# The first two units of a fused attention, mix and expert kernel, written as one fixed list of steps

## The chip, the core and the metric

The kernel runs on one core of a Trainium2 chip. The metric is the time of one execution on the device, in microseconds (us). The engines of the core are named as in the profile: PE (TensorE, matrix products), DVE (VectorE), ACT (ScalarE), POOL (GpSimd) and SP (SyncE, which here only issues transfers). Each engine works through its own list of instructions in order; semaphores hold an instruction back until what it reads is there, or until the buffer that it writes is free.

## What is computed

Three blocks follow each other; everything is float32, but for the three weights `w_k`, `w_v` and `w_r` of the second block, which come as float64.

```python
# 1: attention inside chunks of 64 tokens; q, k, v are 8 x 8 heads x 576 tokens x 64
scores = scale * np.matmul(q_c, k_c.transpose(0, 1, 2, 4, 3))
attn = np.exp(scores - scores.max(-1)); attn /= attn.sum(-1) + 1e-09
x = np.matmul(attn, v_c)                       # -> 8 x 576 x 512
# 2: each token mixed with the one before it, then a gated two-layer net
xk = mu_k * x + (1.0 - mu_k) * x_prev
xr = mu_r * x + (1.0 - mu_r) * x_prev
k = np.maximum(xk @ w_k, 0.0)                  # w_k 512 x 1024
v = k * k @ w_v                                # w_v 1024 x 512
x = v / (1.0 + np.exp(-(xr @ w_r)))            # w_r 512 x 512
# 3: four experts, causal attention each, the two best per token (not touched by the change)
```

## The kernel before

The 4608 tokens are cut into 36 tiles of 128 (two of them are a pair) and into 12 units of 384 tokens (three tiles). Block 1 is done pair by pair: `s_T` transposes a q and a k tile on PE (L148), `s_S` makes the scores of a pair (L185) and its softmax on DVE and ACT (row maximum L190, subtraction L191, exponential L194, sum L196 to L198, multiplication L199), `s_PT` transposes the result and `s_PV` multiplies it with v (L219) and copies it into `XT`, the attention's result of a unit.

Block 2 is done unit by unit. `s_shift` makes the two mixed inputs in four parts of 128 channels: ACT scales the token before (L268), DVE adds the token itself (L269), ACT rounds the sum to the high half (L270), DVE subtracts to get the low half (L271). Every product of this block is taken as three matmuls of 384 columns (high by high, high by low, low by high; L57 to L59 in `mm3`), so a unit takes 48 matmuls for r (4 output blocks), 96 for k (8 blocks) and 96 for v (4 blocks in two halves). The result of k is squared and split by ACT (L294 to L296) and, in the first two units, by DVE (L297).

The float64 weights are turned into pairs of float32 halves while the first units run: 20 chunks of 128 x 512 numbers (4 of `w_r`, 8 of `w_k`, 8 of `w_v`), each loaded as 512 KB of raw words (L328) into the tile `st`. A chunk goes through a chain over three engines: absolute value on ACT (L334), maximum with a small constant on POOL (L335), a shift and two bit operations on DVE (L336 to L338), rounding to the high half on POOL (L46), and the subtraction for the low half on DVE (L348).

What is issued when is set in two steps. The code's order comes from the string `pro` (a chunk `c`, an attention step `a`, loads `q` and `v`) and then from the loop over units, which puts conversions (`early`), attention steps (`rate0`, `rate`) and shifts (`sh`, `sh2`) between the blocks of r, k and v. Then the scheduler of the language reorders instructions inside each engine's list by priority and by its own timing. From unit 2 on there are no conversions any more, only r, k, v, attention and shifts; after unit 11 the experts follow.

Of the kernel before, what the change touches and what calls it, by code (L numbers as in the profile page):

```python
# [61 lines left out]
def attn_mix(tc, at, x2T, q, k, v, mu_k, mu_r, w_k, w_v, w_r, ident, attended_all, mixed_k):  # L62
# [14 lines left out]
    with ExitStack() as ctx:  # L77
# [24 lines left out]
        def load_qk(t):  # L102
            for src, nm in ((q, "q"), (k, "k")):
                if by_dve(t):
# [39 lines left out]
        def to_sbuf(src, nm):  # L144

            p = bank("Tps")
            for g in range(HP):
                nc.tensor.transpose(p[:, g], src[:, g * 128:(g + 1) * 128], ident)  # L148
            o = at.tile([128, HP, 128], F32, tag=nm, bufs=CFG["tb"], name=nm)
            nc.scalar.activation(out=o, in_=p, func=ACTF.Copy)  # L150
            return o

# [15 lines left out]

        def s_S(j):
# [15 lines left out]
            m = at.tile([128, 2, 2, HP], F32, tag="m", name="m")  # L187
            e = at.tile([128, 2, HP, 2, CH], F32, tag="P", name="P")
            for o, p in enumerate(banks):
                nc.vector.tensor_reduce(m[:, o], p, axis=AXX, op=ALU.max)  # L190
                nc.vector.tensor_tensor(e[:, :, :, o], p, m[:, o].unsqueeze(3).to_broadcast([128, 2, HP, CH]),  # L191
                                        op=ALU.subtract)
            ef = e.rearrange("p i g o k -> p (i g o) k")
            nc.scalar.activation(out=ef, in_=ef, func=ACTF.Exp, scale=scale)  # L194
            z = m.rearrange("p o i g -> p (o i g)")
            nc.vector.tensor_reduce(z, ef, axis=AXX, op=ALU.add)  # L196
            nc.vector.tensor_scalar(z, z, 1e-9, None, op0=ALU.add)
            nc.vector.reciprocal(z, z)  # L198
            eng(nc, CFG["amul"][j >= CFG["first_j"]]).tensor_tensor(  # L199
                ef, ef, z.unsqueeze(2).to_broadcast([128, 2 * H, CH]), op=ALU.mult)  # L200
            for i in range(2):
                PP[2 * j + i] = e[:, i]

        def s_PV(j):
            banks = [bank("PVps").rearrange("p g (i k) -> p i g k", i=2) for _ in range(2)]
# [15 lines left out]
            for c, p in enumerate(banks):  # L221

                done = 0
                while done < 2:
# [32 lines left out]
        def s_shift(u, ws, g):  # L257
            x = XT[u]
            now, prev = x[:, g, :, 1:], x[:, g, :, :SEG]
            for w in ws:  # L260
                nm = "kr"[w]
                if g == 0:
                    XS[u, w] = Split(wkr.tile([128, KD, UNIT], F32R, tag="xh" + nm, name="xh" + nm),
                                     wkr.tile([128, KD, UNIT], F32R, tag="xl" + nm, name="xl" + nm))
                o = XS[u, w]
                a = wkr.tile([128, NSEG, SEG], F32, tag="xa", bufs=2, name="xa")
                af = a.rearrange("p s t -> p (s t)")
                nc.scalar.activation(out=a, in_=prev, func=ACTF.Copy, scale=mu1[:, w, g:g + 1])  # L268
                nc.vector.scalar_tensor_tensor(a, now, mu[:, w, g:g + 1], a, op0=ALU.mult, op1=ALU.add)  # L269
                nc.scalar.activation(out=o.hi[:, g], in_=af, func=ACTF.Copy)  # L270
                nc.vector.tensor_tensor(o.lo[:, g], af, f32(o.hi[:, g]), op=ALU.subtract)  # L271
# [6 lines left out]
        def mix_r(u, m):  # L278
            if m == 0:
                sig[u] = mx.tile([128, KD, UNIT], F32, tag="sig", name="sig")  # L280
            p = ps.tile([128, UNIT], F32, tag="mix", bufs=3, name="mps")
            cc = slice(m * 128, (m + 1) * 128)
            mm3(nc, p, [((wr.hi[:, g, cc], wr.lo[:, g, cc]), rhs(XS[u, 1], g)) for g in range(KD)])
            nc.scalar.activation(out=sig[u][:, m], in_=p, func=ACTF.Sigmoid)  # L284

        def mix_k(u, m):
            p = ps.tile([128, UNIT], F32, tag="mix", bufs=3, name="mps")
            cc = slice(m * 128, (m + 1) * 128)
            mm3(nc, p, [((wk.hi[:, g, cc], wk.lo[:, g, cc]), rhs(XS[u, 0], g)) for g in range(KD)])
            o = Split(mx.tile([128, UNIT], F32R, tag="kh", bufs=KF, name="kh"),  # L290
                      mx.tile([128, UNIT], F32R, tag="kl", bufs=KF, name="kl"))
            r2 = wkr.tile([128, UNIT], F32, tag="r2", bufs=2, name="r2")
# [9 lines left out]
        def mix_v(u, m, half):
            if half == 0:
                vps[0] = ps.tile([128, UNIT], F32, tag="mix", bufs=3, name="mps")
            p = vps[0]
            cc = slice(m * 128, (m + 1) * 128)
            gs = range(half * KF // 2, (half + 1) * KF // 2)
            mm3(nc, p, [((wv.hi[:, g, cc], wv.lo[:, g, cc]), (kk[u, g].hi, kk[u, g].lo)) for g in gs],
                first=half == 0, last=half == 1)
            if half:  # L310
                o = mx.tile([128, UNIT], F32, tag="r", bufs=2, name="x2o")
                nc.vector.tensor_tensor(o, p, sig[u][:, m], op=ALU.mult)
                d = mx.tile([128, 2, UNIT], F32R, tag="x2d", bufs=CFG["x2d"], name="x2d")
                copy(nc, CFG["x2hi"], d[:, 0], o)
                eng(nc, CFG["x2lo"]).tensor_tensor(d[:, 1], o, f32(d[:, 0]), op=ALU.subtract)
                nc.gpsimd.dma_start(out=x2T[u * UNIT // (2 * S)][:, cc, u * UNIT % (2 * S):][:, :, :UNIT].rearrange("s p t -> p s t"), in_=d)

        done = [0]

        def conv(src, dst, g, c0, n):  # L320

            i = done[0] - 1
            if i < 4:
# [618 lines left out]
```

## Time and profile before

| | |
|---|---|
| median of 3 runs | 1005.36 us (1004.91 to 1005.54) |
| profiled execution | 1005.0 us, its span in the trace 1003.2 us |
| PE busy | 947.7 us, 94% of the span |
| DVE, ACT, POOL busy | 627.9, 621.0, 323.3 us |
| moved by DMA | 108.42 MB, 108 GB/s over the span |
| the 20 conversions | ACT takes the first chunk at 4.1 us, the last at 110.1 us |

The profiled execution is the one that the rows below come from; what lies between its time and its span is outside the trace. All three runs lie within 0.6 us of each other. A time in a row is counted from the start of the span.

### The profile page before, as it was taken

To read this page: it belongs to the slowest core of one execution; us is meant where nothing else is said; L and a number is where in the kernel's file an instruction comes from. 1 tells how busy PE (TensorE), PEld (TensorE's weight loads), DVE (VectorE), ACT (ScalarE), POOL (GpSimd) and SP (SyncE) were. 2 spreads that over 40 slices of the span, in tenths; PEclk is the share of its full clock that TensorE was granted. 3 is DMA by queue.
4 is the path that set the end of the run, shared out by engine and by line. 5 is a ranking of instruction groups with operands and counts; after the bars stand their busy time and mean duration, and the time that the engine had idled before them with its cause. 6 is when DMAs were issued, how large, how long until landed. Compare 5 with 4: busy or idle time off the path is not lost.

```text
span 1003.2 us, 21781 instructions
## 1 busy us (share of the span) xinstructions
PE 947.7 (94%) x8038; PEld 909.8 (91%) x8038; DVE 627.9 (63%) x1610; ACT 621.0 (62%) x1423; POOL 323.3 (32%) x447
## 2 busy tenths in 40 slices
PE   3669899999999999999999999999999999999997
PEld 2569899999999899999999999988999999989985
DVE  5899935355644655654645220587677867887895
ACT  2478663838474747576575724476676857676674
POOL 5343412333333333343333326423331232233101
PEclk8699999999999999999999999999999999999999
DMA  8785352353425353534213124664452637253412
GB/s 226 184 207 142 95 107 75 53 118 66 112 34 119 62 125 55 123 62 82 69 38 85 32 64 129 124 171 137 120 148 77 181 77 210 61 178 99 136 43 97
DMA packets 218979, 108.42 MB, mean 108 GB/s; under 512 B 182920, under 2 KB 195320, under 8 KB 218872
## 3 DMA queue, kind: packets, MB, share of 16 engines
q1 hardware_dynamic: 188600, 67.16, 29.2%
q0 software_dynamic: 30272, 39.86, 14.6%
q8 instruction: 64, 1.05, 0.5%
q14 instruction: 43, 0.35, 0.1%
HBM read 66.01 MB, written 28.38 MB: 94 GB/s over the span
## 4 chain that ended last, share of the span: by engine, by line
PE 74%; DVE 11%; ACT 6%; DMA 2%; SPq 2%; issue 2%; POOL 1%; DVEq 0%; ACTq 0%; POOLq 0%
PE mps L57 14%; PE mps L59 14%; PE mps L58 14%; PE pj L57 6%; PE pj L59 6%; PE pj L58 6%; PE Sps L645 4%; PE Tps L705 3%; PE AVps L738 2%; PE AVps L734 2%; PE Tps L148 2%; DVE PTl L712 1%; DVE sm L647 1%; DMA st<-in_moe_w_k_dram 1%; DVE xa L269 1%
## 5 line engine op out<-in xcount | busy, mean ns | idle before, releaser
L57 PE MATMUL mps<-xhk,wkh 128*128 128x384 f32 x384 | 131.5, 343 | 2.1 <-ACT r L294 2.1
L297 POOL TENSOR_TENSOR kl<-r,kh 128x384 fp32r<-128x384 f32 x80 | 82.5, 1031 | 148.7 <-ACT kh L296 124.6
L58 PE MATMUL mps<-xlk,wkh 128*128 128x384 f32 x384 | 129.1, 337 | 0.0
L59 PE MATMUL mps<-xhk,wkl 128*128 128x384 f32 x384 | 128.9, 336 | 0.0
L57 PE MATMUL mps<-kh,wvh 128*128 128x384 f32 x384 | 127.3, 339 | 0.4 <-ACT r L294 0.4
L59 PE MATMUL mps<-kh,wvl 128*128 128x384 f32 x384 | 126.2, 335 | 0.9 <-DVE wvl L348 0.9
L58 PE MATMUL mps<-kl,wvh 128*128 128x384 f32 x384 | 126.8, 334 | 0.0
L657 ACT ACTIVATE P<-sm,nm 128x512 f32<-128x512 f32 (+3 forms) x144 | 83.9, 584 | 23.6 <-DVE nm L647 19.7
L647 DVE CUSTOM_DVE_ANT_0 sm<-Sps,mask 128x256 f32<-128x256 f32 (+4 forms) x160 | 74.3, 477 | 22.2 <-PE Sps L645 21.0
L269 DVE SCALAR_TENSOR_TENSOR xa<-XT,mu,xa 128x384 f32<-128x384 f32 x96 | 66.1, 701 | 18.0 <-ACT xa L268 17.8
L57 PEld LDWEIGHTS mps<-xhk,wkh 128*128 128x128 f32 x384 | 72.5, 189 | 3.9 <-ACT r L294 3.2
L712 DVE TENSOR_TENSOR PTl<-Tps,PTh 128x512 fp32r<-128x512 f32 (+2 forms) x144 | 70.7, 504 | 7.0 <-ACT PTh L711 5.6
L57 PEld LDWEIGHTS mps<-kh,wvh 128*128 128x128 f32 x384 | 71.9, 188 | 1.1 <-ACT r L294 0.7
L59 PEld LDWEIGHTS mps<-kh,wvl 128*128 128x128 f32 x384 | 71.7, 188 | 1.2 <-DVE wvl L348 1.2
L58 PEld LDWEIGHTS mps<-xlk,wkh 128*128 128x128 f32 x384 | 72.2, 188 | 0.1
L59 PEld LDWEIGHTS mps<-xhk,wkl 128*128 128x128 f32 x384 | 72.2, 188 | 0.0
L58 PEld LDWEIGHTS mps<-kl,wvh 128*128 128x128 f32 x384 | 72.0, 188 | 0.0
L57 PE MATMUL mps<-xhr,wrh 128*128 128x384 f32 x192 | 66.4, 347 | 3.6 <-ACT sig L284 3.6
L754 POOL TENSOR_TENSOR Yf<-Yf,zb 128x576 f32<-128x576 f32 x14 | 20.0, 1430 | 152.9 <-DVE Yf L749 152.7
L711 ACT ACTIVATE PTh<-Tps 128x512 fp32r<-128x512 f32 (+2 forms) x144 | 62.7, 453 | 8.7 <-PE Tps L705 6.9
L705 PE MATMUL Tps<-ident,P 128*128 128x128 f32 x384 | 63.1, 273 | 2.8 <-DVE PTl L712 1.8
L58 PE MATMUL mps<-xlr,wrh 128*128 128x384 f32 x192 | 65.7, 342 | 0.0
(185 smaller groups left out, 2682.2 us busy)
## 6 DMA issues: line engine op xcount, KB each, us to landing
x2T<-x2d POOLq DMA_DIRECT2D x48, 384.0 KB, 3.2
x<-x2T POOLq DMA_DIRECT2D x32, 576.0 KB, 5.7
K<-Kph SPq DMA_DIRECT2D x64, 128.0 KB
out_dram<-o SPq DMA_DIRECT2D x32, 256.0 KB
ldq<-in_q_dram SPq DMA_DIRECT2D x176, 32.0 KB
ldk<-in_k_dram SPq DMA_DIRECT2D x176, 32.0 KB
ldv<-in_v_dram SPq DMA_DIRECT2D x20, 256.0 KB
st<-in_moe_w_k_dram SPq DMA_DIRECT2D x8, 512.0 KB
```

The costliest lines, as they stand in the source:

```text
L57: nc.tensor.matmul(out=out, lhsT=ah, rhs=bh, start=first and i == 0, stop=False)
L58: nc.tensor.matmul(out=out, lhsT=ah, rhs=bl, start=False, stop=False)
L59: nc.tensor.matmul(out=out, lhsT=al, rhs=bh, start=False, stop=last and i == n - 1)
L148: nc.tensor.transpose(p[:, g], src[:, g * 128:(g + 1) * 128], ident)
L269: nc.vector.scalar_tensor_tensor(a, now, mu[:, w, g:g + 1], a, op0=ALU.mult, op1=ALU.add)
L297: eng(nc, CFG["klo"][u >= CFG["nearly"]]).tensor_tensor(o.lo, r2, f32(o.hi), op=ALU.subtract)
L645: issued = nc.tensor.matmul(out=pp[:, :w], lhsT=x, rhs=y[:, a:a + w], start=n == 0, stop=n == len(terms) - 1)
L647: nc.vector.tensor_tensor_reduce(out=sm[:, a:a + w], in0=pp[:, :w], in1=mk[:, :w], op0=ALU.add, op1=ALU.min, scale=-scale, scalar=3e38, ac ...
L657: nc.scalar.activation(out=x[:, :nk], in_=sm[:, :nk], func=ACTF.Exp, scale=-1.0, bias=nm[:, :1], accum_out=z)
L705: nc.tensor.transpose(pp[:, j], x[:, j * 128:(j + 1) * 128], ident)
L711: nc.scalar.activation(out=h, in_=src, func=ACTF.Copy)
L712: nc.vector.tensor_tensor(l, src, f32(h), op=ALU.subtract)
```

## The change

Units 0 and 1, with the six pairs of attention that come before and beside them, the 20 conversions and the shifts of units 0, 1 and 2, and also unit 2's four blocks of r, are cut into small steps (one load, one transposition, one softmax operation, one matmul group). A string `START` lists these steps; each is issued in the order of the list, and `in_line` ties every instruction to the one before it on its engine, so that the scheduler can't reorder them. Unit 2's other instructions are tied behind the last one of the list. The loop over units starts at unit 2.

The conversion of a chunk is changed as well: the ACT step now scales by a power of two, the maximum on POOL is gone, and the first two DVE steps work on the low words in place, inside the loaded tile `st` (every second word), without waiting for ACT.

```diff
-F64_ZERO = 2.0 ** -15
+F64_BIAS = 2.0 ** -112
+START = """
+L3 L2 L1 L4 lq0 L5 lq1 A3 G3 lk0 lk1 B3 A2 G2 H3 O3 B2 A1 G1 H2 O2 G4 A4 Tq0 B1 Eq0 B4 H1 G5 L10 H4 O1 Tq1 O4 A5 Eq1
...
+FIRST_UNITS, FIRST_PAIRS = 2, 6
...
-            nc.scalar.activation(out=z, in_=f32(h), func=ACTF.Abs)
-            nc.gpsimd.tensor_scalar(z, z, F64_ZERO, None, op0=ALU.max)
-            nc.vector.tensor_scalar(b, b, 3, 0x3FFFFFF8, op0=ALU.logical_shift_left, op1=ALU.bitwise_and)
-            nc.vector.scalar_tensor_tensor(b, l, 29, b, op0=ALU.logical_shift_right, op1=ALU.bitwise_or)
-            nc.vector.scalar_tensor_tensor(b, h, -(1 << 30), b, op0=ALU.bitwise_and, op1=ALU.bitwise_or)
...
+        def c_scale(i):
+            CZ[i] = at.tile([128, n], F32, tag="cz", bufs=2, name="cz")
+            nc.scalar.activation(out=CZ[i], in_=f32(ST[i][0]), func=ACTF.Copy, scale=F64_BIAS)
...
+        def c_bits(i):
+            h, l = ST[i]
+            nc.vector.tensor_scalar(l, l, 29, None, op0=ALU.logical_shift_right)
+            nc.vector.scalar_tensor_tensor(l, h, -(1 << 31), l, op0=ALU.bitwise_and, op1=ALU.bitwise_or)
...
+        def c_join(i):
+            b = CZ[i].bitcast(I32)
+            nc.vector.scalar_tensor_tensor(b, b, 3, ST.pop(i)[1], op0=ALU.logical_shift_left, op1=ALU.bitwise_or)
...
+        stages = dict(
+            L=c_load, A=c_scale, G=c_bits, B=c_join, H=c_hi, O=c_lo,
+            lq=lambda t: load_qk(t, "q"), lk=lambda t: load_qk(t, "k"), lv=load_v,
+            Tq=to_T(qT, "qT"), Tk=to_T(kT, "kT"), Tp=to_T(PT, "PT"),
+            Eq=from_T(qT, "qT"), Ek=from_T(kT, "kT"), Ep=from_T(PT, "PT"),
+            S=s_scores, X=s_max, U=s_sub, E=s_exp, Z=s_sum, Y=s_mul, V=s_products, W=s_result,
+            prev=s_prev, mu=one_less_mu, r=r_mm, s=r_sig, k=k_mm, K=k_act, J=k_lo,
+            v=v_mm, y=v_mul, z=v_hi, x=v_lo, D=v_store)
...
+        def in_line(start, advance=True):
+            for ins in traced[start:]:
+                if ins.engine in last:
+                    tc.add_manual_dep(ins, last[ins.engine].name,
...
+        for s in START:
...
+            in_line(at0)
...
-        for u in range(NU):
+        for u in range(FIRST_UNITS, NU):
```

In the list, `L3` is the load of chunk 3, `A`, `G`, `B`, `H`, `O` are the five parts of its conversion (L444, L448 and L449, L453, the rounding on POOL, L464), `a` to `d` with `k` or `r` the four parts of a shift. The rows below are the engines' lists as they are built; the numbers behind the names tell tiles apart.

DVE's list at its very start, before:

```order
L336 TENSOR_SCALAR cz_100<-cz_100 128x512
L337 SCALAR_TENSOR_TENSOR cz_100<-st_98,cz_100 128x512
L338 SCALAR_TENSOR_TENSOR cz_100<-st_98,cz_100 128x512
L336 TENSOR_SCALAR cz_110<-cz_110 128x512
L337 SCALAR_TENSOR_TENSOR cz_110<-st_108,cz_110 128x512
L338 SCALAR_TENSOR_TENSOR cz_110<-st_108,cz_110 128x512
L348 TENSOR_TENSOR wrl_90<-cz_100,wrh_89 128x512
```

and in the changed kernel (`cz` comes from ACT, `st` from the load):

```order
L448 TENSOR_SCALAR st_97<-st_97 128x512
L449 SCALAR_TENSOR_TENSOR st_97<-st_97 128x512
L453 SCALAR_TENSOR_TENSOR cz_111<-cz_111,st_97 128x512
L448 TENSOR_SCALAR st_99<-st_99 128x512
L449 SCALAR_TENSOR_TENSOR st_99<-st_99 128x512
L464 TENSOR_TENSOR wrl_90<-cz_111,wrh_89 128x512
L453 SCALAR_TENSOR_TENSOR cz_120<-cz_120,st_99 128x512
```

The four DVE operations of a chunk are still one shift, two combined bit operations and one subtraction, but only the third now reads something that ACT made, and none waits for POOL ahead of the rounding.

DVE's list around the last two chunks of `w_v`, whose low halves are the last two rows with `wvl`; before, with the last shift of unit 1 (`XT_542`, `xlk_1145`) and the softmax of the sixth pair (`Sps_1668`, `Sps_1669`) among them:

```order
L269 SCALAR_TENSOR_TENSOR xa_1296<-XT_542,mu_93,xa_1296 128x384
L338 SCALAR_TENSOR_TENSOR cz_828<-st_826,cz_828 128x512
L336 TENSOR_SCALAR cz_859<-cz_859 128x512
L271 TENSOR_TENSOR xlk_1145<-xa_1296,xhk_1144 128x384
L337 SCALAR_TENSOR_TENSOR cz_859<-st_857,cz_859 128x512
L338 SCALAR_TENSOR_TENSOR cz_859<-st_857,cz_859 128x512
L348 TENSOR_TENSOR wvl_92<-cz_828,wvh_91 128x512
L190 TENSOR_REDUCE m_1702<-Sps_1668 128x8
L190 TENSOR_REDUCE m_1702<-Sps_1669 128x8
L191 TENSOR_TENSOR P_1703<-Sps_1668,m_1702 128x8x64
L348 TENSOR_TENSOR wvl_92<-cz_859,wvh_91 128x512
```

and in the changed kernel (`kl` is unit 0's k, `Sps_1289` and `Sps_1290` the sixth pair, `XT_573` unit 1):

```order
L464 TENSOR_TENSOR wvl_92<-cz_1239,wvh_91 128x512
L453 SCALAR_TENSOR_TENSOR cz_1268<-cz_1268,st_1210 128x512
L388 TENSOR_TENSOR kl_1258<-r2_1259,kh_1257 128x384
L388 TENSOR_TENSOR kl_1162<-r2_1163,kh_1161 128x384
L464 TENSOR_TENSOR wvl_92<-cz_1268,wvh_91 128x512
L223 TENSOR_REDUCE m_1361<-Sps_1289 128x8
L223 TENSOR_REDUCE m_1361<-Sps_1290 128x8
L329 SCALAR_TENSOR_TENSOR xa_1006<-XT_573,mu_93,xa_1006 128x384
```

All of unit 1's shifts (eight times L269 and eight times L271 in the list before) and the sixth pair's maximum and subtraction have moved behind the last low half of `w_v`.

SP's list, which issues the loads, at its start, before:

```order
L328 DMA st_118<-in_moe_w_r_dram 128x1024
L118 DMA ldq_128<-in_q_dram 128x8x64
L118 DMA ldk_130<-in_k_dram 128x8x64
L118 DMA ldq_132<-in_q_dram 128x8x64
L118 DMA ldk_134<-in_k_dram 128x8x64
L328 DMA st_172<-in_moe_w_r_dram 128x1024
L134 DMA ldv_227<-in_v_dram 64x4x64 x4
```

and in the changed kernel:

```order
L438 DMA st_101<-in_moe_w_r_dram 128x1024
L438 DMA st_103<-in_moe_w_k_dram 128x1024
L144 DMA ldq_105<-in_q_dram 128x8x64
L438 DMA st_107<-in_moe_w_k_dram 128x1024
L144 DMA ldq_109<-in_q_dram 128x8x64
L144 DMA ldk_115<-in_k_dram 128x8x64
L144 DMA ldk_117<-in_k_dram 128x8x64
L438 DMA st_149<-in_moe_w_k_dram 128x1024
L438 DMA st_170<-in_moe_w_v_dram 128x1024
L160 DMA ldv_174<-in_v_dram 64x4x64 x4
```

Five loads of weights stand ahead of the first k tile where three stood, and two more ahead of the first v tile where one stood; a weight load can only be issued when its `st` buffer is free. Up to and with the twentieth weight load, SP's list holds 37 tiles of q, k or v (256 KB each) before and 36 in the changed kernel.

## Rows read from the trace of the kernel before

**Rows 1.** The page's span in 40 slices, busy tenths.

```profile
PE   3669899999999999999999999999999999999997
DVE  5899935355644655654645220587677867887895
```

**Rows 2.** Busy time by stretch: length, PE, PEld, DVE, ACT, POOL, PEclk, DMA share, GB/s.

```profile
0.00:75.00 75.00, 40.84 (x588) 33.87 (x588) 57.16 (x93) 37.69 (x67) 34.45 (x40) 0.82 0.81 205
0.00:118.90 118.90, 81.44 (x1019) 72.90 (x1020) 99.98 (x164) 70.37 (x134) 52.99 (x56) 0.87 0.68 175
126.65:600.00 473.35, 469.86 (x4174) 462.13 (x4174) 234.18 (x395) 283.40 (x561) 152.27 (x184) 1.00 0.37 78
```

**Rows 3.** Timeline, single instructions: start, length, what.

```profile
4.12 0.66 ACT L334 ACTIVATE cz<-st 128x512 f32<-128x512 f32 x1 [2.10 <-DMA st<-in_moe_w_r_dram]
...
63.74 0.69 PE L57 MATMUL mps<-xhr,wrh 128*128 128x384 f32 x1
...
110.05 0.68 ACT L334 ACTIVATE cz<-st 128x512 f32<-128x512 f32 x1
...
116.44 1.28 DVE L190 TENSOR_REDUCE m<-Sps 128x8 f32<-128x512 f32 x2
...
118.24 0.68 DVE L348 TENSOR_TENSOR wvl<-cz,wvh 128x512 fp32r<-128x512 f32 x1
...
126.65 0.34 PE L57 MATMUL mps<-xhr,wrh 128*128 128x384 f32 x1
...
134.97 0.34 PE L57 MATMUL mps<-xhk,wkh 128*128 128x384 f32 x1
```

**Rows 4.** Waits from 0 to 118.9 us on DVE, ACT, SP: total, times, longest.

```profile
DVE cz L336 <- POOL cz L335: 12.6, 6, 6.4
...
ACT cz L334 <- DMA st<-in_moe_w_k_dram: 12.4, 6, 5.9
...
SPq L328 <- DVE cz L338: 25.3, 10, 6.3
```

**Rows 5.** Groups by shape, 0 to 130 us: busy us, mean ns, idle before.

```profile
L336 DVE TENSOR_SCALAR cz<-cz 128x512 int32<-128x512 int32 x20 | 9.6, 478 | 12.8 <-POOL cz L335 12.6
L337 DVE SCALAR_TENSOR_TENSOR cz<-st,cz 128x512 int32<-128x512 int32 x20 | 14.0, 698 | 0.3
L269 DVE SCALAR_TENSOR_TENSOR xa<-XT,mu,xa 128x384 f32<-128x384 f32 x18 | 11.0, 626 | 0.9 <-ACT xa L268 0.9
L271 DVE TENSOR_TENSOR xlr<-xa,xhr 128x384 fp32r<-128x384 f32 x8 | 5.6, 711 | 1.2 <-ACT xhr L270 1.2
L190 DVE TENSOR_REDUCE m<-Sps 128x8 f32<-128x512 f32 x12 | 7.7, 681 | 0.9 <-PE Sps L185 0.9
L191 DVE TENSOR_TENSOR P<-Sps,m 128x512 f32<-128x512 f32 x12 | 7.9, 680 | 0.0
L297 DVE TENSOR_TENSOR kl<-r,kh 128x384 fp32r<-128x384 f32 x8 | 5.6, 706 | 0.1
L335 POOL TENSOR_SCALAR cz<-cz 128x512 f32<-128x512 f32 x20 | 32.1, 1606 | 36.3 <-ACT cz L334 30.6 <-DVE xlk L271 5.7
```

**Rows 6.** Durations of two DVE lines: ns least, median, most.

```profile
L336 DVE TENSOR_SCALAR cz<-cz x20: 407/418/834, 6.4 to 113.3; 128x512 int32<-128x512 int32 x20
...
L297 DVE TENSOR_TENSOR kl<-r,kh x8: 546/559/965, 91.9 to 107.9; 128x384 fp32r<-128x384 f32 x8
```

**Rows 7.** PE's other pieces: timeline of transpositions, chain at a pair.

```profile
88.47 0.60 PE L148 MATMUL Tps<-ident,ldq 128*128 128x128 f32 x4
88.91 0.27 PE L148 MATMUL Tps<-ident,ldk 128*128 128x128 f32 x1
...
232.36 1.09 PE Sps L182 x64
233.45 1.00 PE PVps L216 x64
```

More of the change, by code (lines that the diff above doesn't have):

```diff
@@ L100, in by_dve, with load_qk @@
             return t >= 2 * CFG["dve_j"]
-        def load_qk(t):
+        def load_qk(t, which="qk"):
             for src, nm in ((q, "q"), (k, "k")):
+                if nm not in which:
+                    continue
                 if by_dve(t):
@@ L276, in rhs, with mix_bank, r_mm, r_sig @@
             return o.hi[:, g], o.lo[:, g]
-        def mix_r(u, m):
+        MB = {}
+        def mix_bank(f, u, m):
+            p = MB[f, u, m] = ps.tile([128, UNIT], F32, tag="mix", bufs=3, name="mps")
+            return p, slice(m * 128, (m + 1) * 128)
+        def r_mm(u, m):
+            p, cc = mix_bank("r", u, m)
+            mm3(nc, p, [((wr.hi[:, g, cc], wr.lo[:, g, cc]), rhs(XS[u, 1], g)) for g in range(KD)])
+        def r_sig(u, m):
             if m == 0:
                 sig[u] = mx.tile([128, KD, UNIT], F32, tag="sig", name="sig")
[L281 to L284, printed above, removed]
@@ L286, in mix_k @@
[L286 to L292 removed]
+            nc.scalar.activation(out=sig[u][:, m], in_=MB.pop(("r", u, m)), func=ACTF.Sigmoid)
@@ L302, in mix_v, with k_lo, mix_k, v_mm @@
[L302 to L306, printed above, removed]
+        def k_lo(u, m):
+            o = kk[u, m]
+            eng(nc, CFG["klo"][u >= CFG["nearly"]]).tensor_tensor(o.lo, K2.pop((u, m)), f32(o.hi), op=ALU.subtract)
+        def mix_k(u, m):
+            k_mm(u, m)
+            k_act(u, m)
+            k_lo(u, m)
+        def v_mm(u, m, half):
+            p, cc = (MB["v", u, m], slice(m * 128, (m + 1) * 128)) if half else mix_bank("v", u, m)
@@ L309, in mix_v, with v_mul, v_hi, v_lo @@
                 first=half == 0, last=half == 1)
-            if half:
[L311 to L322, printed above, removed]
+        X2 = {}
+        def v_mul(u, m):
+            o = mx.tile([128, UNIT], F32, tag="r", bufs=2, name="x2o")
+            nc.vector.tensor_tensor(o, MB.pop(("v", u, m)), sig[u][:, m], op=ALU.mult)
+            X2[u, m] = o, mx.tile([128, 2, UNIT], F32R, tag="x2d", bufs=CFG["x2d"], name="x2d")
+        def v_hi(u, m):
+            o, d = X2[u, m]
+            copy(nc, CFG["x2hi"], d[:, 0], o)
+        def v_lo(u, m):
+            o, d = X2[u, m]
+            eng(nc, CFG["x2lo"]).tensor_tensor(d[:, 1], o, f32(d[:, 0]), op=ALU.subtract)
+        def v_store(u, m):
+            o, d = X2.pop((u, m))
+            cc = slice(m * 128, (m + 1) * 128)
+            nc.gpsimd.dma_start(out=x2T[u * UNIT // (2 * S)][:, cc, u * UNIT % (2 * S):][:, :, :UNIT].rearrange("s p t -> p s t"), in_=d)
+        def mix_v(u, m, half):
+            v_mm(u, m, half)
+            if half:
+                for f in (v_mul, v_hi, v_lo, v_store):
+                    f(u, m)
+        n = CFG["cn"]
+        chunks = [(src, dst, g, c) for src, dst in ((w_r, wr), (w_k, wk), (w_v, wv))
+                  for c in range(0, src.shape[1], n) for g in range(src.shape[0] // 128)]
+        ST, CZ = {}, {}
+        def c_load(i):
+            src, _, g, c = chunks[i]
             if i < 4:
@@ L382, in step @@
             f(x)
-        conv_todo = chunks(w_r, wr) + chunks(w_k, wk) + chunks(w_v, wv)
-        conv_todo.reverse()
-        def convert(n):
-            for _ in range(min(n, len(conv_todo))):
-                done[0] += 1
-                f, *args = conv_todo.pop()
-                f(*args)
-        loads = {"q": iter(range(CFG["ldb"])), "v": iter(range(CFG["vb"]))}
-        def first_shift():
-            for ws in ((1, 0),) if CFG["sh2"][2] >= 0 else ((1,), (0,)):
-                for g in range(KD):
-                    s_shift(0, ws, g)
@@ new lines, in attn_mix @@
+        for i, f in enumerate((shift_prev, shift_now, shift_hi, shift_lo)):
+            for w, nm in enumerate("kr"):
+                stages["abcd"[i] + nm] = lambda u, g, f=f, w=w: f(w, u, g)
+        traced = nc.cur_bb.bb.instructions
+        last = {}
+        def in_line(start, advance=True):
+            for ins in traced[start:]:
+                if ins.engine in last:
+                    tc.add_manual_dep(ins, last[ins.engine].name,
+                                      mybir.DependencyInfo(mybir.DependencyClass.NoSync, mybir.DependencyReason.DATA),
+                                      reason="order of the first units")
+                if advance:
+                    last[ins.engine] = ins
```

205 lines of the change are left out of this document (134 added, 71 removed).

## The prediction

> **What bounds the kernel now.** I read the page's slices first, to see where PE is not busy. PE fills every slice from the fifth on, while DVE is full in slices two to four and falls to half afterwards [rows 1]. A table by stretch says it in numbers: from 126.65 us, where unit 1's r begins, to 600 us, PE is busy 469.9 of 473.35 us, while DVE is busy 234.2 and ACT 283.4 us. From 0 to 118.9 us DVE is busy 99.98 us and PE 81.4 us, at a mean granted clock of 0.87 [rows 2]. So from unit 1 on the kernel runs as fast as PE can, and what can be won lies ahead of that: how soon PE has its first unit behind it. The products are the same before and after, so the whole is decided by the moment at which the same PE work is done.
>
> The moment I use is the first matmul of unit 1's r, at 126.65 us [rows 3]. What holds it up is DVE. v of unit 0 needs all eight chunks of `w_v`, and the low half of the twentieth chunk starts on DVE at 118.24 and takes 0.68 us [rows 3], so it is done at 118.9. By then DVE has been idle 118.9 - 99.98 = 18.9 us. The waits name the reason for most of it: 12.6 us in front of L336, for the maximum on POOL, 6.4 of them at the start [rows 4].
>
> **The change part by part.** *Work moved behind the last chunk.* The lists of DVE show that before the change the eight shift parts of unit 1 and the maximum and subtraction of the sixth pair stood ahead of the last low half, and now stand behind it. These are eight L269 at 0.626, eight L271 at 0.711, two L190 at 0.681 and two L191 at 0.680 us [rows 5]: 5.0 + 5.7 + 1.4 + 1.4 = 13.5 us. Neighbours overlap a little: two L190 of 0.681 are shown as 1.28 us together [rows 3], 0.08 less than their sum. I take that off for each of the 20: 11.9 us. The other work ahead of the last low half is the same by count: 20 chunks, five pairs of softmax, unit 0's shifts and its eight L297. What has moved must still be done before unit 1's r, but beside 84 matmuls of v, where DVE has room (below).
>
> *The conversion's steps.* DVE has one shift, two combined operations and one subtraction per chunk as before. What is new is that the shift works on every second word. The trace has no such one-source operation: L336, of the same size, takes 0.478 on average and 0.418 in the median, L337, which has two sources and reads the same strided words, takes 0.698 [rows 5, 6]. The new shift lies between these, at nothing or at 20 x (0.698 - 0.478) = 4.4 us more. I take nothing, since L336 is the same operation on the same number of elements, and keep 4.4 us for the range.
>
> The Trainium skill, "VectorE: DVE Perf Modes", section "What auto-detection actually checks", has a one-source operation run at two elements per cycle when source and destination are in SBUF and their outer dimensions are even or equal; a step between 32-bit words is not among the conditions. The two durations of L336 and L337 agree with two speeds, but no row here shows a strided one-source operation. By that page the sum stays as it is; were the page wrong there, it would be the 4.4 us.
>
> *POOL.* The maximum L335 goes: 20 times, 32.1 us [rows 5], out of POOL's 53.0 us up to 118.9 [rows 2]. POOL is not the bound; what counts is the link in the chain, and the longer durations that DVE shows beside POOL. L336 and L297 lie on average above their medians by 0.060 and 0.147 us [rows 5, 6], which over 20 and 8 of them is 1.2 + 1.2 = 2.4 us. That POOL causes it the trace does not show; it could be 0. I take it in proportion to POOL's work that goes, 32.1 / 53.0 of 2.4, or 1.5 us.
>
> *DVE's idle time.* Of the 12.6 us in front of L336 the start will remain up to the first load: ACT takes it at 4.12 us [rows 3], and DVE can now do so at the same time, so 4.2 us of the first 6.4 stay. The other 6.2 us are five waits, of at most 6.2 / 5 = 1.2 us on average, while the link that goes is one POOL operation of 1.6 us [rows 5]; so I take them as gone. The remaining 18.9 - 12.6 = 6.3 us (waits on PE, on ACT, on the rounding) I leave. Idle after the change: 6.3 + 4.2 = 10.5 us.
>
> *Loads.* SP's list now has weights further ahead. Up to the twentieth weight load it holds 20 x 512 KB + 36 x 256 KB = 19.9 MB (20.2 before). In the first 75 us, 205 GB/s were moved, with the DMA engines busy 0.81 of the time [rows 2]; at that rate the last load lands at 97 us, and without pauses (205 / 0.81 = 253 GB/s) at 79. The sum below needs it at 94.4 (97.1 less 2.7, below), so the loads are close to being the bound.
>
> *The sum.* The last low half is done at 99.98 - 11.9 - 1.5 + 10.5 = 97.1 us. After it PE has at most the rest of unit 0's v, 84 matmuls. 48 matmuls of r take 134.97 - 126.65 = 8.32 us [rows 3], 0.173 each, so this is 14.6 us. In the lists up to 12 transpositions, one pair's scores and one pair's products stand in the same place: four transpositions take 88.91 - 88.47 = 0.44 us, so 1.3 us, and 1.09 + 1.00 us for the pair [rows 7]. Together 18.0 us, and unit 1's r begins at 115.1 us. On DVE the moved 11.9 us and unit 0's last steps stand beside these 18.0 us and fit. Before, PE had done ten more transpositions at that moment (1.1 us), so the 126.65 is to be compared as 125.55. The gain is 10.4 us. The profiled execution took 1005.0 us, so 994.6; the median of the runs is 0.4 us above it, which gives **995.0 us**.
>
> *Costs at nothing.* Unit 0's k and its eight L297 are on DVE as before. Four blocks of unit 2's r now stand inside the list, behind unit 1's v; PE is full there and has the same work. After unit 2 the lists follow the old rules, with six pairs done, where the old one had six pairs of scores and nearly six of products. What covers this is PE's full stretch [rows 2]; if the cover went, each pair of attention would cost its own 2.1 us [rows 7] once.
>
> **The rivals.** *The waits were for the loads.* ACT waited 12.4 us for chunks of `w_k` to land [rows 4]. If DVE, with POOL out of its way, now waits for the loads themselves, the 6.2 us stay, and the gain is 4.2: 1001.2 us. For it speaks the DMA share of 0.81, against it that SP stood 25.3 us waiting for L338 to free a buffer [rows 4], so that loads were also late because DVE was.
>
> *Slower: the loads come no faster.* Before, ACT took the last chunk at 110.05 us [rows 3], 20.2 MB in 110 us, or 183 GB/s. If the changed list, in which a weight load that waits for its `st` buffer holds back every q, k and v load behind it, keeps that pace, its last chunk comes at 109 us. Scaling, joining, rounding and subtracting then need some 2.7 us (four operations near 0.68), so the last low half is done at 111.7, unit 1's r begins at 129.7, 4.2 us late: 1009.6 us. This decides from a landing at 125.55 - 18.0 - 2.7 = 104.9 us, a pace of 190 GB/s. Against it: the DMA engines were busy only 0.68 of the time up to 118.9 us [rows 2], so the old pace was set by buffers, and these come free with DVE.
>
> *No change.* PE begins its full stretch earlier and another engine then holds it back by as much: 1005.4 us. With DVE and ACT at 234 and 283 of 473 us [rows 2] I see no candidate.
>
> *More.* If nearly all idle time but the start goes (4.2 us left) the gain is 16.7: 988.7 us. A list that fixes the order can also place a step badly, and then every engine stands in line behind it; so I don't take this as likely.
>
> **How the numbers follow.** I give the forecast (987 to 1000) 0.62, the waits for loads (1000 to 1003.3) 0.18, no change 0.07, slower 0.13. A difference under 0.2%, 2 us, can't be told from none here. So faster 0.80, same 0.07, slower 0.13. The likeliest alone is 988 to 1000: at its upper end stands the strided shift with its 4.4 us, at its lower end the case with little idle time. The range must reach into the other cases; from 987 to 1004 leaves some 0.05 below and 0.14 above.
>
> **What the profile will show.** Right: the first matmul of unit 1's r near 115 us; the last `wvl` done near 97; DVE's idle time before it near 10 us, and none of it for POOL ahead of the first shift; L448 at 0.42 to 0.48 us; PE full from unit 1's r to 600 us. Wrong: L448 near 0.7; long waits of L453 on ACT or of ACT's L444 on loads after 30 us; SP standing at a weight load while q, k or v is what DVE's or PE's next step needs; or a PE gap in units 1 to 3 that was not there.

## The result and the profile after

The changed kernel takes 996.19 us (median of 4 runs, 994.85 to 997.61), the kernel before, measured beside it, 1005.13 us (4 runs, 1003.11 to 1005.54). The ratio is 0.9915, 95% interval 0.9896 to 0.9934: 8.9 us faster. The forecast was 995.0 us. The profiled execution took 996.1 us, its span is 994.1 us; times below are counted from its start.

The slices of the page, to be read against [rows 1]:

```profile
PE   2779999999999999999999999999999999999997
DVE  6979834446653656554645310688677776877895
```

The third slice of PE rises from 6 to 7, the fifth from 8 to 9: from the fourth slice (of 25 us) on PE is full. The table by stretch (columns as in [rows 2]) shows the same and holds the two stretches of the sum, up to the end of the last low half of `w_v` and from there to unit 1's r:

```profile
0.00:75.00 75.00, 43.81 (x688) 37.19 (x692) 61.24 (x102) 44.12 (x79) 13.79 (x27) 0.85 0.88 215
0.00:118.90 118.90, 86.01 (x1096) 78.54 (x1097) 102.46 (x174) 75.84 (x140) 26.44 (x43) 0.90 0.75 190
0.00:102.45 102.45, 69.56 (x1000) 62.12 (x1001) 86.70 (x145) 67.01 (x124) 21.08 (x36) 0.88 0.81 202
102.45:116.85 14.40, 14.40 (x86) 14.37 (x85) 13.93 (x27) 7.39 (x15) 4.61 (x8) 1.00 0.39 101
126.65:600.00 473.35, 469.31 (x4177) 462.11 (x4176) 235.23 (x391) 291.26 (x572) 153.78 (x184) 1.00 0.35 75
```

Up to 118.9 us POOL is busy 26.4 us, half of before's [rows 2], PE 4.6 us more, and 22.6 MB were moved (118.9 us at 190 GB/s) where it was 20.8 MB. From 126.65 to 600 us PE's busy time differs by 0.6 us. The single instructions that [rows 3] show of before, from the timeline of the changed kernel:

```profile
57.99 0.44 PE L81 MATMUL mps<-xhr,wrh 128*128 128x384 f32 x1
...
98.86 0.66 ACT L444 ACTIVATE cz<-st 128x512 f32<-128x512 f32 x1
...
101.77 0.68 DVE L464 TENSOR_TENSOR wvl<-cz,wvh 128x512 fp32r<-128x512 f32 x1
...
116.85 0.34 PE L81 MATMUL mps<-xhr,wrh 128*128 128x384 f32 x1
...
125.17 0.34 PE L81 MATMUL mps<-xhk,wkh 128*128 128x384 f32 x1
```

Unit 0's r begins 5.8 us earlier, the last chunk reaches ACT 11.2 us earlier, the last low half is done at 102.45 instead of 118.9 us, and unit 1's r begins at 116.85 instead of 126.65 us. Counted at equal PE work (125.55, as in the prediction) that is 8.7 us. The last matmul of the kernel begins at 989.5 us, before at 998.2: the lead is the same 8.7 us at the end, so nothing of it is given back later.

The waits of DVE up to 102.45 us and of SP up to 105 us answer to [rows 4]:

```profile
DVE st L448 <- DMA st<-in_moe_w_r_dram: 4.2, 1, 4.2
DVE st L448 <- DMA st<-in_moe_w_v_dram: 3.5, 3, 2.0
DVE st L448 <- DMA st<-in_moe_w_k_dram: 2.1, 2, 1.6
DVE wkl L464 <- POOL wkh L70: 1.2, 2, 0.7
DVE kl L388 <- ACT kh L384: 1.2, 1, 1.2
...
SPq L438 <- DVE cz L453: 13.5, 6, 3.7
```

The 12.6 us for POOL are gone; 4.2 us at the start stay, and a new wait stands in their place: 5.6 us for chunks of `w_v` and `w_k` to land. At its weight loads SP waits 13.5 us for L453 to free a buffer, where it waited 25.3 us for L338; with the shorter waits for other DVE steps at the same line (2.1, 1.9 and four under 0.8) it is 19.5 us.

What PE waits for between 58 us and unit 1's r, and the instructions around its last wait:

```profile
PE Tps L173 <- DMA ldk<-in_k_dram: 3.9, 1, 3.9
PE Sps L213 <- ACT qT L178: 1.7, 1, 1.7
```

```profile
98.86 0.66 ACT L444 ACTIVATE cz<-st 128x512 f32<-128x512 f32 x1
99.43 0.58 ACT L178 ACTIVATE qT<-Tps 128x512 f32<-128x512 f32 x1
...
100.06 0.69 PE L213 MATMUL Sps<-kT,qT 64*64 64x64 f32 x32 [1.70 <-ACT qT L178]
...
103.75 0.33 PE L83 MATMUL mps<-kh,wvl 128*128 128x384 f32 x1
```

The matmul at 103.75 us is the first that reads the last low half, which is done at 102.45: PE does not stand for it, there are 1.3 us to spare. What PE last stands for is `qT`, which ACT copies right behind its scaling of the last chunk. From 100.06 us on PE works without a pause into unit 1's r. DVE is still part of that chain: ACT had waited for a `kl` of DVE three times between 89 and 96 us, 2.0 us in all.

The groups by shape from 0 to 130 us, against [rows 5]:

```profile
L449 DVE SCALAR_TENSOR_TENSOR st<-st 128x512 int32<-128x512 int32 x20 | 15.3, 765 | 0.7
...
L448 DVE TENSOR_SCALAR st<-st 128x512 int32<-128x512 int32 x20 | 9.0, 451 | 10.0 <-DMA st<-in_moe_w_r_dram 4.2 <-DMA st<-in_moe_w_v_dram 3.5 <-DMA st<-in_moe_w_k_dram 2.1
...
L388 DVE TENSOR_TENSOR kl<-r,kh 128x384 fp32r<-128x384 f32 x9 | 5.7, 641 | 7.0 <-ACT kh L384 7.0
...
L340 DVE TENSOR_TENSOR xlr<-xa,xhr 128x384 fp32r<-128x384 f32 x8 | 4.2, 543 | 0.7 <-ACT xhr L336 0.7
```

The strided shift L448 takes 0.451 us, as L336 did (0.478); L340, the old L271, fell from 0.711 to 0.543.

### The profile page after: what moved, and what is told of

Read it like the earlier page. It is cut to its first block, busy times and chain, and to the rows that moved or that the text cites. A ratio compares the mean times of both kernels' runs of the same rounds, so it can differ in the third digit from the quotient of the medians.

```text
span 994.1 us, 21728 instructions
## 1 busy us (share of the span) xinstructions
PE 943.7 (95%) x8038; PEld 908.0 (91%) x8038; DVE 628.0 (63%) x1610; ACT 627.5 (63%) x1425; POOL 293.1 (29%) x427
## 4 chain that ended last, share of the span: by engine, by line
PE 78%; DVE 10%; DMA 4%; ACT 3%; issue 2%; SPq 1%; POOL 1%; DVEq 0%; ACTq 0%; POOLq 0%
PE mps L81 15%; PE mps L83 15%; PE mps L82 15%; PE pj L81 6%; PE pj L83 6%; PE pj L82 6%; PE Sps L777 4%; PE Tps L837 3%; PE AVps L870 2%; PE Tps L173 2%; PE AVps L866 2%; DMA st<-in_moe_w_k_dram 2%; DVE PTl L844 1%; DVE sm L779 1%; PE Sps L210 1%
## 5 line engine op out<-in xcount | busy, mean ns | idle before, releaser
L329 DVE SCALAR_TENSOR_TENSOR xa<-XT,mu,xa 128x384 f32<-128x384 f32 x96 | 68.5, 728 | 24.2 <-ACT xa L325 24.1
L325 ACT ACTIVATE xa<-XT,mu 128x384 f32<-128x384 f32 x96 | 57.2, 613 | 12.4 <-DVE xlr L340 9.8
```

The source lines that it names most:

```text
L325: nc.scalar.activation(out=a, in_=XT[u][:, g, :, :SEG], func=ACTF.Copy, scale=mu1[:, w, g:g + 1])
L329: nc.vector.scalar_tensor_tensor(a, XT[u][:, g, :, 1:], mu[:, w, g:g + 1], a, op0=ALU.mult, op1=ALU.add)
```

## The experiments

**Which half of the change it is.** The theory: DVE's order around the last chunks and the shorter conversion both give a part. The list was run with the old conversion, the scheduler's order with the new one, and the list with nothing that ties its steps.

The list with the old conversion:

```diff
-nc.scalar.activation(out=CZ[i], in_=f32(ST[i][0]), func=ACTF.Copy, scale=F64_BIAS)
+nc.scalar.activation(out=CZ[i], in_=f32(ST[i][0]), func=ACTF.Abs)
+nc.gpsimd.tensor_scalar(CZ[i], CZ[i], F64_ZERO, None, op0=ALU.max)
```

(and the three old DVE steps); the kernel before with the new conversion:

```diff
-nc.gpsimd.tensor_scalar(z, z, F64_ZERO, None, op0=ALU.max)
+nc.vector.tensor_scalar(l, l, 29, None, op0=ALU.logical_shift_right)
```

(and the other new steps); the list without ties:

```diff
-if ins.engine in last:
+if False and ins.engine in last:
```

> The list with the old conversion (absolute value on ACT, maximum on POOL, then the three DVE steps in a row where the list has the joining step). Theory: the gain of 8.9 us comes mostly from the order, since the moved 11.9 us of DVE work does not depend on the conversion; lost are 2.2 us at the start (6.4 in place of 4.2 us until DVE's first step), 1.5 us of longer DVE durations beside POOL, and up to 5 us because each chunk's chain is 1.6 us longer in a list timed for the shorter one: 998 to 1003 us. Rival A, the conversion is the whole gain: 1005. Rival B, the order is the whole gain: 996.

> The kernel before with the new conversion alone, the order left to the scheduler. Theory: DVE's idle time in front of the first conversion step falls from 12.6 us to the 4.2 of the start and what the loads then cost, while unit 1's shifts stay wherever the scheduler puts them: 1000 to 1004 us. Rival A, the conversion is the whole gain: 996. Rival B, the order is the whole gain: 1005.

> The changed kernel with the steps issued in the order of the list, but without the ties, so that the scheduler reorders them again. Theory: what counts is DVE's order around the last chunks of the weights; the scheduler will move some of it back, and the time lies between: 998 to 1003 us. Rival: the order in which the code is written is enough, 995 to 997.5.

Measured against 1006.06 us of before: the list with the old conversion 1020.01 us (ratio 1.0141, 1.0128 to 1.0154), the old order with the new conversion 1007.28 us (1.0015, 1.0003 to 1.0028), the list without ties 1024.36 us (1.0179, 1.0164 to 1.0195). All three forecasts were missed on the slow side: neither half alone gains anything, and two of the three lose more than the whole change gains. What ended DVE's, PE's and SP's idle time in the three (list with old conversion to 125 us; old order with new conversion to 125 us; list without ties to 136 us):

```profile
DVE cz L454 <- POOL cz L446: 19.1, 14, 6.9
...
SPq L439 <- DVE cz L456: 29.7, 8, 6.2
```

```profile
DVE st L335 <- DMA st<-in_moe_w_k_dram: 7.4, 7, 2.3
DVE st L335 <- DMA st<-in_moe_w_r_dram: 5.9, 3, 4.2
...
SPq L118 <- PE Tps L148: 15.9, 6, 10.5
```

```profile
PE PVps L278 <- ACT PT L178: 9.5, 4, 6.9
...
SPq L144 <- PE Tps L173: 15.4, 6, 11.5
```

The list was laid out for a chain without POOL. With POOL's maximum in it, DVE stands 19.1 us in line for it (12.6 in the scheduler's order), buffers come free later, SP waits 29.7 us for them, and unit 1's r begins at 136.2 us, 10.6 later than before at equal PE work (125.55); the rest of the 14 us is lost behind the list. In the scheduler's order the new conversion takes the wait for POOL away, and DVE waits for the loads: SP stands 15.9 us (10.3 in the kernel before) at q or k tiles whose buffer PE has not freed, with the weights behind them. Unit 1's r begins there at 121.4 us, but with 29 transpositions, one pair's scores and one pair's products less done than in the kernel before, which is 29 x 0.11 + 1.09 + 1.00 = 5.3 us [rows 7]: 126.7 against 126.65 us, no gain at equal work. Without ties the scheduler puts the same steps into another order, and SP stands 11.5 us at one load; which of its waits makes the 18 us no run shows.

**The moved work put back.** Unit 1's shifts went back ahead of the last chunks, for r behind `dk0,3`, for k behind `k0,7`; all other steps keep their order, and the PE list is the changed kernel's, matmul for matmul.

```diff
-V4 O19 X5 v0,0,1 lv10 W4 br1,2 prev2 U5 cr1,2 v0,1,0 lv11 br1,0 E5 dr1,2
+V4 O19 X5 v0,0,1 lv10 W4 prev2 U5 v0,1,0 lv11 E5
...
-dk0,3
+dk0,3 ar1,2 ar1,0 br1,2 br1,0 cr1,2 cr1,0 dr1,2 dr1,0 ar1,3 ar1,1
...
-k0,7
+k0,7 ak1,2 ak1,1 bk1,2 bk1,1 ck1,2 ck1,1 dk1,2 dk1,1 ak1,3 ak1,0
...
```

> The changed kernel with unit 1's shifts put back ahead of the last chunks in the list (those for r behind unit 0's shifts, those for k behind unit 0's last block of k). Eight L329 at 0.62 and eight L340 at 0.59 us, 9.7 us of DVE work, now stand ahead of the last low half. Theory: DVE is what holds up unit 1's r, and of the 9.7 us only what DVE had idle there (loads and ACT, some 5 us) is absorbed: last low half 5 to 10 us later, 1001 to 1006 us. Rival: by then the loads hold DVE up, so that the work fits into idle time: 996 to 998.

Measured 1007.78 us (1.0019, 1.0009 to 1.0028): the whole gain is gone, and nearly 2 us more than expected at most. The table by stretch:

```profile
100.00:125.00 25.00, 19.00 (x216) 18.54 (x215) 19.42 (x34) 11.67 (x24) 5.22 (x9) 0.86 0.39 103
```

and the last low half, from the timeline:

```profile
112.14 0.68 DVE L445 TENSOR_TENSOR wvl<-cz,wvh 128x512 fp32r<-128x512 f32 x1
```

The last low half is done at 112.8 us, 10.4 later for 9.7 us of work, unit 1's r begins 12.4 us later (129.2) and the last matmul 12.6 us later. PE stands for the same `qT`, which comes 10.35 us later than in the changed kernel:

```profile
110.41 1.14 PE L194 MATMUL Sps<-kT,qT 64*64 64x64 f32 x32 [6.00 <-ACT qT L159]
```

The other 2.0 us are lost behind this wait: from 110.4 to 115.0 us the granted clock is 0.50, where the changed kernel has 1.00 behind its wait of 1.7 us. So the place of these shifts is the step that makes the gain. Their scaling and rounding on ACT moved with the work on DVE, and the run does not part the two engines.

**Are the loads in the sum?** Tiles 0 to 5 got one load for q and k, and pairs one v tile for both halves: 2.36 MB less, the engines' instructions unchanged.

```diff
+                if t < 6 and t in SEEN:
+                    qkv[nm, t] = SEEN[t]
+                    continue
...
+            if t < 6 and ("v", t ^ 1) in qkv:
+                qkv["v", t] = qkv["v", t ^ 1]
+                return
```

> The changed kernel with fewer loaded bytes: for tiles 0 to 5 one loaded tile serves as q and as k, and one v tile serves both tiles of a pair, 2.36 MB fewer before 50 us; every engine's instructions are unchanged (the attention of these tiles is computed on repeated data). Theory (of DVE's 15.75 us of idle time before the last low half 5.6 us are waits for loads, the step of the prediction that was too small): at 218 GB/s the 2.36 MB are some 10 us of loading; DVE's waits for the loaded st tiles beyond the first fall from 5.6 to under 2 us, unit 0's r begins 3 to 6 us earlier, the last low half is done at 97 to 100 us, and the time is 991 to 994 us. Rival (what holds DVE are other links, and the loads fill time that would be waited anyway): the last low half stays at 101 to 103 us and the time at 995.5 to 997.5 us.

**Is POOL's work a price by itself, and does DVE's work set the pace?** One kernel does the old maximum beside the chain, with each chunk's scaling:

```diff
+            nc.gpsimd.tensor_scalar(beside, beside, 1.0, None, op0=ALU.max)
```

Two give low halves to POOL, five (chunks 12, 13, 14, 15, 18) or nine (5, 6, 7, 10 as well):

```diff
-            nc.vector.tensor_tensor(lo, CZ.pop(i), f32(hi), op=ALU.subtract)
+            e = nc.gpsimd if i in (12, 13, 14, 15, 18) else nc.vector
+            e.tensor_tensor(lo, CZ.pop(i), f32(hi), op=ALU.subtract)
```

> The changed kernel with the old maximum on POOL put back beside the chain: 20 times the same operation of 128x512 on a tile of its own, which nothing reads, issued with each chunk's scaling. Theory (POOL's work lengthens DVE's, the term of 1.5 us): DVE's busy time up to the last low half rises from 86.7 us by 1 to 3 us, and the time by 1 to 3 us, to 997 to 999 us. Rival (what the old maximum cost was only its place in the chain): DVE's busy time stays within 0.5 us and the time within 1 us of the changed kernel's.

> The changed kernel with the low half of five of the eight chunks of w_v (not the last two, which the first v waits for) subtracted by POOL and not by DVE, in the same places of the list. Theory (DVE's work up to the last low half sets the start of unit 1's r, and each us off it moves that start): 5 x 0.68 = 3.4 us leave DVE, of which 0 to 1.5 us come back through longer DVE operations and later cz buffers; the last low half is done 1 to 3.4 us earlier and the time is 993 to 995.5 us. Rival (the loads set the pace, DVE's freed time becomes waiting for st tiles): no gain, 995.5 to 997.5 us, with DVE's waits for loads 2 to 3 us longer.

> As the run with five low halves on POOL, with those of four chunks of w_k as well, nine in all. Theory (DVE's work sets the pace): 9 x 0.68 = 6.1 us leave DVE, 0 to 2.5 us come back; the time is 990.5 to 995 us and below the run with five. Rival (the loads set the pace): 995.5 to 997.5 us; or slower, where POOL's slower subtraction holds a cz buffer that ACT's next scaling needs: ACT's wait for cz at L444 grows beyond its 3.8 us and the time is over 998 us.

Measured beside 1005.93 us: fewer bytes 998.30 us (0.9929, 0.9915 to 0.9942), POOL beside the chain 1006.28 (1.0004, 0.9996 to 1.0013), five low halves on POOL 1009.80 (1.0038, 1.0021 to 1.0055), nine 1010.59 (1.0047, 1.0034 to 1.0060). All four missed, and all four for a reason that no theory had named. With fewer bytes unit 1's r began at 114.6 us, 2.3 earlier than in the changed kernel, and with nine low halves at 116.9 us, yet both ended later. The loss stands in unit 3's v, behind the list: from its first matmul to unit 4's r the changed kernel takes 17.4 us (236.4 to 253.8), these four 22.8 to 24.2. The two with low halves on POOL lose 5.7 us more in unit 5's k (25.0 us from its first matmul to that of v, 19.3 in the changed kernel). In the run with fewer bytes the waits and the table by stretch show why:

```profile
PE mps L81 <- ACT kh L391: 3.7, 1, 3.7
```

```profile
234.00:242.00 8.00, 6.20 (x36) 5.87 (x34) 6.68 (x10) 4.59 (x11) 2.31 (x2) 1.00 0.62 116
242.00:250.00 8.00, 6.12 (x19) 6.12 (x20) 6.75 (x12) 6.50 (x13) 1.40 (x2) 0.57 0.43 67
```

PE waits 3.7 us for a `kh` of unit 3, and from 242 to 250 us, where the first 1.9 us are the end of that wait, the granted clock is 0.57 in the mean, so most of that stretch runs at the lower of its two levels, 1.2 GHz: 19 matmuls stand there, 50 in the table of the run below. Where the list ends, the order is the scheduler's again, and it differs: with nine low halves on POOL, 41 of PE's matmuls (transpositions among them) in units 3 to 7 stand elsewhere than in the changed kernel. The kernel with five was left at that; its profiled execution took 1014.2 us, 4.4 over its median, so its other milestones aren't used. The other three were run again with the order behind the list (units 2 to 10) tied to the changed kernel's on every engine; PE's and ACT's lists then are the changed kernel's. (The first of the expectations below says unit 2 where the stall is in unit 3.)

> The run with fewer loaded bytes (one tile serves as q and k, one v tile serves a pair, for tiles 0 to 5), and behind the list, in units 2 to 10, every engine's order is fixed to the one that the changed kernel has there. In the run without that fix unit 1's r began 2.3 us earlier than in the changed kernel, but PE then stood 3.7 us in unit 2's v for ACT's kh, with a granted clock near 0.5 behind it, which the changed kernel doesn't show. Theory (that stall comes of another order behind the list, and the loads do cost time at the start): the stall is gone and the time is 992.5 to 995 us. Rival (the stall comes of the data's earlier arrival, not of the order): PE stands there again and the time is 997 to 999.5 us.

> The run with the old maximum on POOL beside the chain, with the order behind the list fixed in the same way. Theory (POOL's work beside DVE costs what unit 1's r showed, 3.5 us, and the rest of the 10 us was another order behind the list): 998.5 to 1001 us. Rival (all of it is POOL's work): 1004 to 1007 us.

> The run with nine low halves on POOL, with the order behind the list fixed in the same way. In the run without it unit 1's r began at 116.9 us, as in the changed kernel, although DVE had 6.1 us less to do. Theory (DVE and the loads bind together up to the last low half, so relief for DVE alone gives nothing, and the loss was the order behind the list): 995 to 997.5 us. Rival (DVE's relief does give time in most executions): 991 to 994.5 us; or the loss was POOL's: over 1003 us.

Measured beside 1005.74 us: fewer bytes 992.71 us (0.9877, 0.9861 to 0.9892), POOL beside the chain 999.42 (0.9941, 0.9924 to 0.9957), nine low halves 995.81 (0.9903, 0.9888 to 0.9918), each inside its theory's range. The kernel with nine runs from unit 1's r on as the changed kernel does (116.8 and 116.85 us there, the last matmul at 989.6 and 989.5), so the ties by themselves cost nothing that shows. The stall is gone; the same 16 us with fewer bytes:

```profile
232.50:240.50 8.00, 8.00 (x48) 8.00 (x47) 7.72 (x12) 6.23 (x11) 3.17 (x2) 1.00 0.60 114
240.50:248.50 8.00, 8.00 (x50) 7.97 (x49) 7.81 (x16) 5.48 (x10) 2.25 (x5) 1.00 0.45 71
```

So the loads do cost time: with 2.36 MB less the kernel is 3.5 us below the changed one (996.19), and its last low half is done at 98.6 us. A start of unit 1's r is read from one execution: kernels with the same list have it at 114.6 and 113.0 us with fewer bytes, at 120.3 and 121.8 with POOL's maximum, so differences near 1.5 us in it are not to be built on. POOL's maximum beside the chain costs 3.2 us (the intervals of the two ratios touch, but each of its 4 runs is longer than each of the changed kernel's 4); DVE's busy time up to its last low half is 93.35 us, 6.65 more than 86.70. The groups of that run that grew most, beside POOL's:

```profile
L460 DVE SCALAR_TENSOR_TENSOR st<-st 128x512 int32<-128x512 int32 x20 | 17.0, 850 | 0.7
...
L475 DVE TENSOR_TENSOR wrl<-cz,wrh 128x512 fp32r<-128x512 f32 x4 | 4.0, 988 | 0.0
...
L454 POOL TENSOR_SCALAR beside<-beside 128x512 f32<-128x512 f32 x20 | 33.0, 1651 | 0.2
```

For the nine low halves the theory gave the right time for a wrong reason. DVE's busy time up to the last low half is 86.57 us, no less than the changed kernel's 86.70, though 9 x 0.68 = 6.1 us left it: the time did not turn into waits for loads, most of it came back in longer operations, 4.5 us in the two conversion steps alone. Least, median and most of these two steps in that run (in the changed kernel L448 364/422/837 and L449 692/694/983):

```profile
L456 DVE TENSOR_SCALAR st<-st x20: 365/426/1523, 4.7 to 96.4; 128x512 int32<-128x512 int32 x20
...
L457 DVE SCALAR_TENSOR_TENSOR st<-st x20: 694/698/1670, 5.2 to 96.9; 128x512 int32<-128x512 int32 x20
```

The medians stand still, and single operations, more than twice as long, carry it. The last low half is done at 101.04 us all the same, 1.4 us earlier, and yet unit 1's r begins where it did. PE's wait and the table by stretch, here and in the changed kernel, show why:

```profile
98.63 1.14 PE L221 MATMUL Sps<-kT,qT 64*64 64x64 f32 x32 [2.75 <-ACT qT L186]
```

```profile
98.63:102.00 3.37, 3.37 (x98) 3.25 (x99) 3.37 (x6) 0.93 (x3) 1.94 (x3) 0.50 0.19 44
```

```profile
100.06:103.00 2.94, 2.94 (x103) 2.77 (x104) 2.94 (x6) 1.65 (x5) 1.98 (x4) 1.00 0.37 83
```

In this execution PE goes on 1.43 us earlier, after a wait of 2.75 us and not 1.70, and then works at a granted clock of 0.50: from there to unit 1's r it takes 18.14 us, in the changed kernel 16.79.

**Two loads earlier.** DVE's waits for loads had two places: 2.0 us for chunk 15 and 1.6 us for chunk 11, which SP had issued behind v tiles. They were moved ahead of these.

```diff
-...lk9 W1 Z2 lv5 ... dr0,0 L15 Ep4 ... prev1 lv6 A15 ... bk0,0 L11 H15 ...
+...lk9 W1 Z2 L15 lv5 ... dr0,0 Ep4 ... prev1 L11 lv6 A15 ... bk0,0 H15 ...
```

> The changed kernel with two entries of the list moved ahead: the load of chunk 15 (w_v) ahead of the v loads of tiles 5 and 4, and the load of chunk 11 (w_k) ahead of the v load of tile 6; the order behind the list is fixed to the changed kernel's. Its output is the reference's. DVE stood 2.0 us at 58.7 us and 1.6 us at 69.7 us for just these two loads, which SP had issued behind 4 and 8 parts of v tiles. Theory (these waits are part of the chain to the last low half): both waits go, unit 1's r begins 2 to 3.5 us earlier, 992.5 to 994.5 us. Rival (the v tiles, now later, or the next buffers take their place): 995 to 998 us.

Measured 994.27 us (994.15 to 994.58; ratio 0.9889, 0.9872 to 0.9905), 1.9 us below the changed kernel's median; the two intervals overlap, but each of its 4 runs is shorter than each of the changed kernel's 4. DVE's waits for loads after the start are down from 5.6 us to some 1.4:

```profile
DVE st L456 <- DMA st<-in_moe_w_r_dram: 5.0, 2, 4.5
...
DVE st L456 <- DMA st<-in_moe_w_k_dram: 0.6, 1, 0.6
...
DVE st L456 <- DMA st<-in_moe_w_v_dram: 0.3, 1, 0.3
```

and the last low half, from the timeline, is done at 99.78 us, 2.7 earlier:

```profile
99.10 0.68 DVE L472 TENSOR_TENSOR wvl<-cz,wvh 128x512 fp32r<-128x512 f32 x1
```

Unit 1's r begins at 114.2 us, 2.7 earlier. This is the fastest kernel of the study that computes the reference.

## Why the prediction was right, step by step

**The moment that decides.** Right. The gain at unit 1's r, 8.7 us, is the gain at the last matmul and, within 0.3 us, of the median. That PE is held up there by the last low half itself is not what the changed kernel's trace shows: PE stands for ACT's `qT` behind the last chunk, and the low half comes 1.3 us before it is read. Both hang on DVE's work, so the sum by DVE still came near. (The slices of [rows 1] were read one too early: PE's fifth is 8 and its sixth 9, and DVE is near full up to the fifth. Nothing in the sum rests on it.)

**DVE's work up to the last low half.** The prediction's 99.98 - 11.9 - 1.5 = 86.6 us came out as 86.70. That the order makes it, and not only goes with it, is shown by the shifts put back, on ACT as on DVE: 9.7 us of DVE's work cost 12.4 us at unit 1's r. One reading in it was high: 0.711 us is the mean of the L271 for r, those for k took 0.652 in the same trace, so the moved work was some 0.2 us less. The share of 1.5 us for POOL fitted only as part of this sum. POOL's maximum in the changed order costs 6.65 us of DVE; in the kernel before, DVE stood still for part of its time [rows 4], so less of it may have lain beside DVE's work; no run shows how much.

**DVE's idle time.** This is the term that was mis-sized: 10.5 us predicted, 102.45 - 86.70 = 15.75 measured. The start (4.2) and the rest (15.75 - 4.2 - 5.6 = 5.95 for 6.3) are as predicted. The step "so I take them as gone" was wrong: in place of the 6.2 us of waits for POOL stand 5.6 us for the loads. That is the rival on the loads, in its mechanism and nearly in its size. Fewer bytes and the two loads moved ahead show that these waits are part of the time: 3.5 and 1.9 us. The last `wvl` near 97 us and an idle time near 10 us, two of the signs of being right, did not come.

**From the last low half to unit 1's r.** "At most" 18.0 us, measured 14.40 with PE busy throughout. Of v 82 matmuls were left, nearly the 84 of the sum; but the pair's scores and products and eight of the twelve transpositions, 3.0 us in the sum's prices, were done before the last low half. These 3.6 us pay for most of the 5.3 us above: 102.45 + 14.40 = 116.85 stands against 115.1, 1.75 us late. That the two errors lie in opposite directions is luck; with the first alone the forecast would have been 5 us early.

**The strided shift.** Taken like L336, and so it is: 0.451 us in the mean, 0.422 in the median, the two-source L449 on the same words 0.694. The upper bound of 4.4 us did not come. The Trainium skill, "VectorE: DVE Perf Modes", section "What auto-detection actually checks", leaves a step between 32-bit words out of its conditions for a one-source operation, and the trace agrees: 0.422 us against L336's 0.418 [rows 6].

**The slower rival.** The last chunk reached ACT at 98.86 us and not at the 109 us of the old pace: SP's waits for DVE at the weight loads fell from 25.3 to 19.5 us, in the direction that the argument against that rival had.

**What I took at nothing.** Behind the list PE stays full (469.3 of 473.35 us), so this held. But it holds for this list: four runs that changed little before unit 1 lost 5 to 7 us in unit 3's v, because the scheduler's order behind the list changed with it. The prediction had no such case among its rivals.

**The two halves.** The sum took the moved work and the shorter conversion as two terms that add. The runs show that they don't: the one alone loses 14 us (10.6 of them by unit 1's r), the other 1.2, both together gain 8.9. The forecast held because both were there.

## What to carry to other kernels

A fixed order is worth as much as the chain that it was laid out for: judge an order and the operations in it together, since either alone can lose. Where a wait for one engine goes, look at once which load comes due behind it, and move that load in the queue's order, not only the work. And when a small edit ahead of a scheduled stretch changes the end time, compare the milestones and the order behind it before the edit is blamed.

## What the runs showed of the hardware beyond that

POOL's work lengthens single DVE operations and leaves the others alone: L464's `wrl`, 0.681 us at most in the changed kernel, took 1.09 us in the median of 4 beside the maximum; 33.0 us of POOL cost DVE 6.65 us, 0.2 us for each us. Up to 130 us of that run every DVE operation that took over 1.2 times the least of its kind, 32 of them, lay beside an operation on POOL; of the other 146, 45% did. Nine subtractions on POOL took 12.1 us (4 at 1.27, 5 at 1.40) and left DVE's busy time 0.13 us shorter.

A stall of PE can cost more than its length. With fewer bytes and the order not fixed, a wait of 3.7 us in unit 3's v was followed by this stretch:

```profile
244.00:250.00 6.00, 6.00 (x19) 6.00 (x20) 5.37 (x10) 4.50 (x9) 1.30 (x2) 0.51 0.43 67
```

The granted clock, 1.00 before the wait, is 0.51, and that unit's v took 24.2 us and not 17.4, 6.7 us more for a wait of 3.7. The same holds on a smaller scale for `qT` inside unit 0's v: behind waits of 2.75 us (nine low halves) and 6.0 us (shifts put back) the granted clock was 0.50, behind those of 1.70 us (changed kernel) and 1.4 us (two loads earlier) it stayed at 1.00.
